# A kernel's instruction order from a new list scheduler: measured latencies, overlap, the shared port, and a local search

## The chip, the cores and the metric

One core of a Trainium2 chip. The metric is device microseconds of one execution; most executions of one kernel agree within 0.3%. All runs compared below are in the fast state, at a granted TensorE clock of 1.00, but for one repeat that ran once and whose state is therefore unknown.

## The reference

Four residual blocks over `x` of shape (1, 2048, 512), all bfloat16: linear attention with a softmax feature map, then a gated feed-forward, and both again.

```python
def A(x, wqkv, w_phi, wo):                    # 32 heads of 16
    q, k, v = split_heads(x @ wqkv)
    phi = lambda t: concat([softmax(t @ w_phi), softmax(-(t @ w_phi))])
    kv, z = phi(k).T @ v, phi(k).sum(over s)
    return merge_heads((phi(q) @ kv) / (phi(q) @ z + 1e-6)) @ wo
def B(x, W_gate, W_up, W_down):               # F = 1376
    return (relu(x @ W_gate) * (x @ W_up)) @ W_down
x = x + A(layernorm(x)); x = x + B(layernorm(x))
x = x + A(layernorm(x)); x = x + B(layernorm(x))
```

## The kernel before

The kernel writes a list of 3691 operations with reads and writes. A scheduler puts them into one fixed order per engine; waits on semaphores are then derived from the dependences. The engines are in order, so an operation whose data is late holds all that follows on its engine.

```python
class Program:
    ...                                   # the kernel sets SYNC_LAT = 120, SAME_LAT = 60
    DMA_FIXED = 2000.0
    DMA_BW = 240.0
    TRIALS = 6
    def schedule(self):
        ...
        noise = [[rng.uniform(0.92, 1.08) for _ in ops] for _ in range(self.TRIALS)]
        for weight in self.ORDER_WEIGHTS:
            prio = [weight * o.idx - rank[o.idx] - o.boost for o in ops]
            for _ in range(self.PASSES):
                start, finish, order = self._forward(prio)
                span = self._replay(order, noise)      # mean over six noisy replays
                ...
    def _forward(self, prio):
            ...
            if o.is_dma:                  # every DMA, a transpose too, shares one queue
                q_free = max(st + self.DMA_FIXED * 0.35, q_free) + o.dma_bytes / self.DMA_BW
                finish[i] = q_free + self.DMA_FIXED * 0.65
```

A layer's attention first runs the K/V stage (key and value projections, the softmax normalisation on GpSimd, and the sums that give `kv`; in the first layer up to about 55 us), then turns to the "num" stage (`phi(q) @ kv`) and the output projection. A tile is 128 of the 2048 rows: "tile 10" is `yT` of tile 10, "`oT` 4" the attention output of tile 4.

The DMA transposes are 92 in all. Each layer-normalised tile of 128 rows is transposed from `ytile` into `yT`, each attention output from `osb` into `oT` (the first few `yT` tiles are transposed on TensorE instead). The next matmul that reads the tile cannot start before the whole transpose has landed.

```python
    def dma_tr(self, fn, reads, writes, name):
        o = self.prog.dma("sp", fn, reads, writes, 131072, name)
        o.dur = 1190.0
        return o
    ...                                       # K and V projections of tile tt
    op("pe", ... e.matmul(k.pb[bank][:], k.yT[:, ic, tt * 128:(tt + 1) * 128], W[:, ic, :], ...)
    ...                                       # attention tile t: transpose, output projection
    self.dma_tr(lambda e: e.dma_start_transpose(k.oT[:, ob, :, :], k.osb[:, b, :]), ..., f"{tag} otr {t}")
    op("pe", ... e.matmul(k.pb[bank][:], k.oT[:, ob, c, :], k.wo_p[:, c, :], ...)
```

The softmax here doesn't subtract the row's maximum and nothing guards it: scores larger than these inputs give would overflow.

Of the kernel before, what the change touches and what calls it, by code (L numbers as in the profile page):

```python
# [24 lines left out]
class Op:  # L25
    __slots__ = ("idx", "eng", "fn", "reads", "writes", "dur", "is_dma", "queue",
                 "dma_bytes", "deps", "order_deps", "dset", "start", "finish", "cnt", "name", "boost")

    def __init__(self, idx, eng, fn, reads, writes, dur, name="", is_dma=False, queue=None, dma_bytes=0):
        self.idx = idx  # L30
        self.eng = eng
        self.fn = fn
        self.reads = reads
        self.writes = writes
        self.dur = dur
        self.name = name
        self.is_dma = is_dma
        self.queue = queue
        self.dma_bytes = dma_bytes
        self.deps = []  # L40
        self.order_deps = []
        self.start = None
        self.finish = None
        self.cnt = None
        self.boost = 0.0


class Program:
    SYNC_LAT = 500.0
    SAME_LAT = 500.0  # L50
    DMA_FIXED = 2000.0
    DMA_TAIL = 1300.0
    ORDER_WEIGHTS = (5.0, 10.0, 20.0, 30.0)
    PASSES = 12
    TRIALS = 6
    DMA_BW = 240.0
    DMA_ISSUE = {"sp": 650.0, "act": 650.0, "pool": 1100.0}

    def __init__(self, nc, window=48, n_dma_sems=48):
        self.nc = nc  # L60
        self.ops = []
        self.window = window if isinstance(window, dict) else {e: window for e in ENG_NAMES}
        self.n_dma_sems = n_dma_sems

    def op(self, eng, fn, reads=(), writes=(), dur=100.0, name=""):
        assert eng in ENG_NAMES
        o = Op(len(self.ops), eng, fn, list(reads), list(writes), float(dur), name)
        self.ops.append(o)
        return o

    def dma(self, eng, fn, reads=(), writes=(), nbytes=0, name=""):
        assert eng in QUEUE_OF
        o = Op(len(self.ops), eng, fn, list(reads), list(writes), self.DMA_ISSUE[eng], name,
               is_dma=True, queue=QUEUE_OF[eng], dma_bytes=nbytes)
        self.ops.append(o)
# [38 lines left out]
    def schedule(self):  # L114
# [9 lines left out]

        def lat(a, b):
            if a.is_dma:
                return self.DMA_TAIL + self.SYNC_LAT
            if a.eng == b.eng:
                return 0.0 if a.eng == "pe" else self.SAME_LAT
            return self.SYNC_LAT  # L130

        rank = [0.0] * n
        for o in reversed(ops):
            rank[o.idx] = o.dur + max([rank[q] + lat(o, ops[q]) for q, _ in self.succ[o.idx]], default=0.0)
        rng = random.Random(1)
        noise = [[rng.uniform(0.92, 1.08) for _ in ops] for _ in range(self.TRIALS)]
        best = None
        for weight in self.ORDER_WEIGHTS:
            prio = [weight * o.idx - rank[o.idx] - o.boost for o in ops]
            for _ in range(self.PASSES):  # L140
                start, finish, order = self._forward(prio)
                span = self._replay(order, noise)
                if best is None or span < best[0]:
                    best = (span, start, finish, order)
                prio = [t - o.boost for t, o in zip(self._backward(start, finish), ops)]
        _, start, finish, order = best
        self.makespan = max(finish)
        for o in ops:
            o.start, o.finish = start[o.idx], finish[o.idx]
        self.order = [ops[i] for i in order]  # L150
        return self.order


    def _forward(self, prio):
        ops, succ = self.ops, self.succ
# [5 lines left out]
        place = {}  # L161
# [5 lines left out]
        q_free = 0.0  # L167
        first = {e: 0 for e in ENG_NAMES}
# [3 lines left out]
        start, finish, order = [0.0] * n, [0.0] * n, []  # L172
        nxt = {e: None for e in ENG_NAMES}
        dirty = set(ENG_NAMES)
        while len(order) < n:
            for e in dirty:
                lst = pending[e]
                while first[e] < len(lst) and done[lst[first[e]]]:
                    first[e] += 1
                lim = first[e] + self.window[e]  # L180
                nxt[e] = min([(max(free[e], t), prio[i], i) for i, t in avail[e].items() if place[i] < lim], default=None)
            dirty = set()
            keys = [k for k in nxt.values() if k is not None]
            assert keys, "scheduler deadlock"
            st, _, i = min(keys)
            o = ops[i]
            start[i] = st
            free[o.eng] = st + o.dur
            if o.is_dma:
                q_free = max(st + self.DMA_FIXED * 0.35, q_free) + o.dma_bytes / self.DMA_BW  # L190
                finish[i] = q_free + self.DMA_FIXED * 0.65
            else:
                finish[i] = st + o.dur
            done[i] = True
            del avail[o.eng][i]
            dirty.add(o.eng)
            order.append(i)
            for q, is_data in succ[i]:
                e = ops[q].eng
                npred[q] -= 1  # L200
                if is_data:
                    ready[q] = max(ready[q], finish[i] + (self.SAME_LAT if o.eng == e else self.SYNC_LAT))
                if npred[q] == 0:
                    avail[e][q] = ready[q]
                    dirty.add(e)
        return start, finish, order


    def _replay(self, order, noise):
        ops = self.ops  # L210
        total = 0.0
        for f in noise:
            free = {e: 0.0 for e in ENG_NAMES}
            fin = [0.0] * len(ops)
            q_free = 0.0
            for i in order:
                o = ops[i]
                t = free[o.eng]
                for d in o.deps:
                    t = max(t, fin[d] + (self.SAME_LAT if ops[d].eng == o.eng else self.SYNC_LAT))  # L220
                free[o.eng] = t + o.dur * f[i]
                if o.is_dma:
                    q_free = max(t + self.DMA_FIXED * 0.35, q_free) + o.dma_bytes / self.DMA_BW * (3 * f[i] - 2)
                    fin[i] = q_free + self.DMA_FIXED * 0.65 * (5 * f[i] - 4)
                else:
                    fin[i] = free[o.eng]
            total += max(fin)
        return total / len(noise)


    def _backward(self, start, finish):
        ops, succ = self.ops, self.succ
# [12 lines left out]
        for _ in range(n):  # L245
            for e in dirty:
                nxt[e] = min([(-min(late[i] - (finish[i] - start[i]) + ops[i].dur, free[e]), -finish[i], i) for i in avail[e]], default=None)
# [3 lines left out]
            out[i] = free[o.eng] = -k - o.dur  # L251
            avail[o.eng].remove(i)
            dirty.add(o.eng)
            for d in o.deps + o.order_deps:
                e = ops[d].eng
                nsucc[d] -= 1
                lat = 0.0 if d not in o.dset else self.SAME_LAT if e == o.eng else self.SYNC_LAT
                late[d] = min(late[d], out[i] - lat)
# [110 lines left out]
class Kernel:  # L369
    def __init__(self, nc, A_x, A_wqkv, A_w_phi, A_wo, B_W_gate, B_W_up, B_W_down, out):  # L370
        self.nc = nc
        self.prog = Program(nc, window=WINDOW)
        self.prog.SYNC_LAT = 120.0
        self.prog.SAME_LAT = 60.0
        self.prog.DMA_ISSUE = {"sp": 450.0, "act": 500.0, "pool": 1100.0}
# [10 lines left out]
    def op(self, eng, fn, reads, writes, dur, name=""):  # L386
        return self.prog.op(eng, fn, reads, writes, dur, name)

    def dma(self, eng, fn, reads, writes, nbytes, name=""):
        return self.prog.dma(eng, fn, reads, writes, nbytes, name)  # L390

    def dma_tr(self, fn, reads, writes, name):
        o = self.prog.dma("sp", fn, reads, writes, 131072, name)
        o.dur = 1190.0
# [53 lines left out]
    def setup(self):  # L448
# [24 lines left out]
        def ldx(t0, t1, after=()):  # L473
            dma("sp", lambda e: e.dma_start(k.x_sb[:, t0:t1, :], xv[:, t0:t1, :]), list(after), [r("x", t) for t in range(t0, t1)], 131072 * (t1 - t0) if t1 > t0 + 1 else 96000, f"dma x{t0}")
        dma("sp", lambda e: e.dma_start(k.phi_c[:], A_w_phi.rearrange("(kc hl) d f -> (hl d) kc f", hl=8)), [], [r("phi_c")], 16384, "dma phi")
        for ic in range(NC):
            dma("act", (lambda ic: lambda e: e.dma_start(wk_n[:, ic, :], A_wqkv[ic * 128:(ic + 1) * 128, 512:1024]))(ic), [], [R_wkn[ic]], 96000, f"dma wk{ic}")
# [4 lines left out]
        dma("sp", lambda e: e.dma_start(k.wv_p[:], wqkv_v[:, :, 1024:1536]), first, [r("wv", ic) for ic in range(NC)], 524288, "dma wv")  # L482
# [3 lines left out]
        o.dur = 7000.0  # L486
# [92 lines left out]
    def ln(self, t, tag, on_act=False, pe_bank=None, stats=True, copy_act=False):  # L579
# [4 lines left out]
        if tag == "L0" and t > 3:  # L584
# [6 lines left out]
            else:  # L591
                op(how, lambda e: e.tensor_scalar(k.ytile[:, yb, :], k.x_sb[:, t, :], k.rstd[:, t, :], k.nmr[:, t, :], op0=ALU.mult, op1=ALU.add), dep, dst, 407 if how == "dve" else 2090, f"{tag} apply {t}")
        else:
            op("dve", lambda e: e.tensor_scalar(k.ytile[:, yb, :], k.x_sb[:, t, :], k.mv[:, t, 0:1], k.rstd[:, t, :], op0=ALU.subtract, op1=ALU.mult),
               [r("x", t), r("mv", t), r("rstd", t)], [r("yt", yb)], 407, f"{tag} apply {t}")
# [30 lines left out]
    def knorm(self, t, tag):  # L626
# [6 lines left out]
        for eng, s0, s1 in parts:  # L633
# [5 lines left out]
               (1930 if s1 - s0 == 2 else 980) if eng == "pool" else 1050, f"{tag} phik {t} {s0}")  # L639
# [56 lines left out]
    def num(self, t, nring, wring, tag):  # L696
# [3 lines left out]
        for gb in range(3):  # L700
# [18 lines left out]
           RN, [r("zm", b, 0), r("zm", b, 1)], 222 if sm == "dve" else 310, f"{tag} zm {t}")  # L719
        op(sm, lambda e: e.tensor_tensor(k.zd[:, b, :], k.zm[:, b, 0:32], k.zm[:, b, 32:64], ALU.add), [r("zm", b, 0), r("zm", b, 1)], [r("zd", b)], 190 if sm == "dve" else 270, f"{tag} zd {t}")  # L720
# [4 lines left out]
           RN + [r("zr", b)], [r("ab", b, 0), r("ab", b, 1)], 222 if sm == "dve" else 310, f"{tag} ab {t}")  # L725
# [4 lines left out]
           RN + [r("ab", b, 0), r("ab", b, 1)], [r("tsc", b)], 690, f"{tag} tsc {t}")  # L730
        op(sm, lambda e: e.tensor_tensor(k.osb[:, b, :], k.tsc[:, b, 0:512], k.tsc[:, b, 512:1024], ALU.add),  # L731
           [r("tsc", b)], [r("osb", b)], 418 if sm == "dve" else 1160, f"{tag} o {t}")
# [239 lines left out]
```

## Time and profile before

| | before |
|---|---|
| time, median of 3 runs | 391.79 us (391.71 to 392.03) |
| span of the profiled run, clock | 390.3 us, 1.00 |
| TensorE: 2331 matmuls at their pace (estimate from start-to-start gaps) | 373.1 us |
| TensorE stalls: start-to-start gaps less the pace | 11.3 us |

The busy share of TensorE (97%) includes each matmul's drain, so I count stalls instead: the time between the starts of two consecutive matmuls, less the pace of the first (216 ns for 512 columns, 109 for 256, 63 for 144, 56 for 128 and 129). By stretch this gives 5.7 us in the first 20 us, 1.6 from 20 to 50, 1.3 from 50 to 60, 1.2 from 60 to 80, 0.2 from 80 to 240, 1.2 from 240 to 270, 0.1 after.

From the page of the kernel before: the span, the TensorE row (busy us, share, instructions), and the chain of work that ended last.

```profile
span 390.3 us, 6397 instructions
...
PE 379.4 (97%) x2331; PEld 208.0 (53%) x2331; DVE 272.0 (70%) x547; ACT 206.6 (53%) x389; POOL 168.5 (43%) x284
...
PE 88%; POOL 4%; ACT 3%; DMA 2%; DVE 1%; issue 1%; ACTq 0%; POOLq 0%
```

The waits of TensorE in the kernel before (who waited for whom: us in total, times, longest):

```profile
PE ps L509 <- DMA hT<-in_A_wqkv_dram: 3.6, 2, 3.2
PE ps L617 <- ACT yT L605: 1.0, 1, 1.0
...
PE ps L663 <- POOL expk L634: 0.6, 1, 0.6
PE ps L706 <- ACT numbf L366: 0.5, 1, 0.5
...
PE ps L758 <- DMA yT<-ytile: 0.2, 1, 0.2
```

From the groups of the kernel before, GpSimd's normalisation in the K/V stages of both layers (count | busy us, mean ns | idle before it and its releaser):

```profile
L634 POOL TENSOR_TENSOR expk<-expk,rZk 128x1024 bf16<-128x1024 bf16 (+1 forms) x32 | 59.5, 1878 | 37.1 <-DVE rZk L631 19.7
```

### The profile page before, as it was taken

Reading aid. Unit: us, or ns where it says so; the run is one execution under the profiler, and the core shown is the slowest. Engines: PE = TensorE matmul, PEld = TensorE weight load, DVE = VectorE, ACT = ScalarE, POOL = GpSimd, SP = SyncE. Lnnn points to the kernel's source line nnn. Section 1 sums busy time; section 2 is a strip of 40 time slices with the busy share of each in tenths; the row PEclk is TensorE's granted clock in tenths of the full one; section 3 lists DMA queues with packets and bytes.
Section 4 is the critical chain, followed back from the end, with each engine's and each line's share of the span. In section 5 each row is a group of like instructions: output and inputs, shape, how many; then the busy total and the mean of one; then the engine's idle time right before and its main releaser. Section 6 shows DMA issues by size and latency. Waiting matters only on the chain.

```text
span 390.3 us, 6397 instructions
## 1 busy us (share of the span) xinstructions
PE 379.4 (97%) x2331; PEld 208.0 (53%) x2331; DVE 272.0 (70%) x547; ACT 206.6 (53%) x389; POOL 168.5 (43%) x284
## 2 busy tenths in 40 slices
PE   5999989999999999999999999999999999999997
PEld 3445554667644544444444457567774554444444
DVE  4999978877766888866766777897986776232222
ACT  5898859834633404533453484985563462553340
POOL 5499936641724363372244543584553242100000
DMA  6833682311311322401000110132323132100002
GB/s 179 228 67 71 191 299 53 69 40 32 53 40 27 43 55 44 84 10 28 14 15 0 27 29 3 40 80 57 55 55 69 27 42 67 29 14 27 17 12 67
DMA packets 61663, 23.01 MB, mean 59 GB/s; under 512 B 53472, under 2 KB 60608, under 8 KB 61632
## 3 DMA queue, kind: packets, MB, share of 16 engines
q1 hardware_dynamic: 60912, 22.02, 24.4%
q10 hardware_dynamic: 720, 0.59, 0.5%
q8 instruction: 18, 0.29, 0.3%
q14 instruction: 13, 0.11, 0.1%
HBM read 7.91 MB, written 2.10 MB: 26 GB/s over the span
## 4 chain that ended last, share of the span: by engine, by line
PE 88%; POOL 4%; ACT 3%; DMA 2%; DVE 1%; issue 1%; ACTq 0%; POOLq 0%
PE ps L758 39%; PE ps L785 19%; PE ps L617 7%; PE ps L737 7%; PE ps L690 6%; PE ps L706 4%; PE ps L663 3%; PE ps L648 2%; POOL expk L634 2%; ACT expq L693 2%; DVE stats L551 1%; DMA x_sb<-in_A_x_dram 1%; DMA hT<-in_A_wqkv_dram 1%; ACT expk L620 1%; POOL rstd L576 1%
## 5 line engine op out<-in xcount | busy, mean ns | idle before, releaser
L758 PE MATMUL ps<-yT,Wg 128*128 128x512 bf16 (+3 forms) x440 | 130.1, 337 | 0.5 <-DMA yT<-ytile 0.2
L758 PE MATMUL ps<-yT,Wu 128*128 128x512 bf16 (+3 forms) x440 | 129.6, 336 | 0.0
L760 ACT ACTIVATE gate_sb<-ps 128x512 bf16<-128x512 f32 (+3 forms) x110 | 55.9, 512 | 105.3 <-PE ps L758 102.9
L785 PE MATMUL ps<-Wd,hT 128*128 128x512 bf16 (+2 forms) x363 | 106.8, 373 | 0.0
L634 POOL TENSOR_TENSOR expk<-expk,rZk 128x1024 bf16<-128x1024 bf16 (+1 forms) x32 | 59.5, 1878 | 37.1 <-DVE rZk L631 19.7
L758 PEld LDWEIGHTS ps<-yT,Wg 128*128 128x128 bf16 (+1 forms) x440 | 43.4, 100 | 33.8 <-issue 1.1
L758 PEld LDWEIGHTS ps<-yT,Wu 128*128 128x128 bf16 (+1 forms) x440 | 43.7, 100 | 32.6 <-ACT expk L765 0.2
L767 DVE TENSOR_TENSOR hT<-gate_sb,expk 128x512 bf16<-128x512 bf16 (+3 forms) x73 | 29.8, 409 | 37.9 <-ACT expk L765 33.0
L785 PEld LDWEIGHTS ps<-Wd,hT 128*128 128x128 bf16 (+1 forms) x363 | 35.3, 98 | 36.6 <-DVE x_sb L787 0.6
L551 DVE BATCH_NORM_STATS2 stats<-x_sb 128x6 f32<-128x512 bf16 x64 | 42.6, 682 | 5.5 <-DMA x_sb<-in_A_x_dram 5.1
L366 ACT ACTIVATE numbf<-ps 128x432 bf16<-128x432 f32 x64 | 33.1, 536 | 19.5 <-PE ps L706 19.4
L629 DVE TENSOR_REDUCE Zk<-expk 128x64 f32<-128x1024 bf16 x32 | 37.7, 1194 | 5.7 <-ACT expk L620 5.4
L731 POOL TENSOR_TENSOR osb<-tsc 128x512 bf16<-128x512 bf16 x28 | 32.5, 1162 | 19.9 <-DVE tsc L726 17.8
L737 PE MATMUL ps<-wo_p,oT 128*128 128x512 bf16 x128 | 39.8, 379 | 0.0
L770 DVE TENSOR_TENSOR hT<-gate_sb,ps 128x512 bf16<-128x512 bf16 (+2 forms) x37 | 22.7, 613 | 20.8 <-PE ps L758 19.6
L693 ACT ACTIVATE expq<-ps 128x1024 bf16<-128x1024 f32 (+1 forms) x40 | 32.6, 861 | 7.3 <-PE ps L690 7.0
L765 ACT ACTIVATE expk<-ps 128x512 bf16<-128x512 f32 (+3 forms) x73 | 36.1, 497 | 0.1
L706 PE MATMUL ps<-kvbd,expq 128*128 128x144 bf16 x256 | 35.0, 226 | 0.5 <-ACT numbf L366 0.5
L620 ACT ACTIVATE expk<-ps 128x512 bf16<-128x512 f32 x44 | 23.9, 598 | 21.5 <-PE ps L617 21.2
L690 PE MATMUL ps<-yT,Wqp 128*128 128x512 bf16 x128 | 34.6, 379 | 0.6 <-ACT expq L693 0.5
L787 DVE TENSOR_TENSOR x_sb<-x_sb,ps 128x512 bf16<-128x512 bf16 (+1 forms) x33 | 22.0, 669 | 18.8 <-PE ps L785 18.4
L559 POOL TENSOR_TENSOR rstd<-rv,mhalf 128x1 f32<-128x1 f32 (+1 forms) x53 | 31.9, 607 | 2.9
(73 smaller groups left out, 429.2 us busy)
## 6 DMA issues: line engine op xcount, KB each, us to landing
out_dram<-x_sb SPq DMA_DIRECT2D x15, 128.0 KB, 1.7
x_sb<-in_A_x_dram SPq DMA_DIRECT2D x3, 512.0 KB, 6.2
Wu<-in_B_W_up_dram SPq DMA_DIRECT2D x4, 344.0 KB, 5.9
Wg<-in_B_W_gate_dram SPq DMA_DIRECT2D x4, 344.0 KB, 5.5
Wd<-in_B_W_down_dram SPq DMA_DIRECT2D x5, 256.0 KB, 6.9
yT<-ytile SPq DMA_TRANSPOSE x60, 2.5
hT<-in_A_wqkv_dram ACTq DMA_DIRECT2D x4, 128.0 KB, 3.1
x_sb<-in_A_x_dram SPq DMA_DIRECT2D x4, 128.0 KB, 3.7
```

What stands on the lines that cost most here:

```text
L366: return e.activation(out, in_, ACT.Copy) if hasattr(e, "activation") else e.tensor_copy(out, in_)
L551: op("dve", (lambda t: lambda e: e.bn_stats(k.stats6[:, t, :], k.x_sb[:, t, :]))(t), [r("x", t)], [r("st", t)], 685, f"{tag} stats {t}")
L629: op("dve", lambda e: e.tensor_reduce(k.Zk[:, zb, :], k.expk[:, t, :, :].rearrange("p s (h f) -> p (s h) f", f=16), AX.X, ALU.add), [r("ex ...
L634: op(eng, (lambda s0, s1: lambda e: e.tensor_tensor(k.expk[:, t, s0:s1, :].rearrange("p s (h f) -> p (s h) f", f=16), k.expk[:, t, s0:s1, ...
L690: op("pe", (lambda c, ic, bank: lambda e: e.matmul(k.pb[bank][:], k.Wqp[:, ic, c * 128:(c + 1) * 128], k.yT[:, ic, st * 512:(st + 1) * 512 ...
L693: op("act", (lambda c0, s, b0: lambda e: e.activation(k.expq[:, st, c0:c0 + w, s, :], k.ps[:, b0:b0 + w, :], ACT.Exp, scale=(1.0 - 2.0 * s ...
L706: op("pe", (lambda s, c, j, g0, bank: lambda e: e.matmul(k.pb[bank][:, j * GW:(j + 1) * GW], k.expq[:, st, c, s, tt * 128:(tt + 1) * 128], ...
L737: op("pe", (lambda c, bank: lambda e: e.matmul(k.pb[bank][:], k.oT[:, ob, c, :], k.wo_p[:, c, :], start=(c == 0), stop=(c == NC - 1)))(c, ...
L758: op("pe", (lambda bank, W, ic, fc, Mf: lambda e: e.matmul(k.pb[bank][0:Mf, 0:n], W[:, ic, fc * 128:fc * 128 + Mf], k.yT[:, ic, c0:c0 + n] ...
L760: op("act", (lambda Mf, gb, gs: lambda e: e.activation(k.gate_sb[0:Mf, gs, 0:n], k.pb[gb][0:Mf, 0:n], ACT.Relu))(Mf, gb, gs), [self.RP[gb] ...
L765: op("act", (lambda Mf, ub, tu: lambda e: e.activation(k.expk[0:Mf, tu, 0, 0:n], k.pb[ub][0:Mf, 0:n], ACT.Copy))(Mf, ub, tu), [self.RP[ub] ...
L785: op("pe", (lambda fc, Kf, u, c0, bank, m0, m1: lambda e: e.matmul(k.pb[bank][:, m0:m1], k.hT[0:Kf, u, c0:c0 + 128], k.Wd[0:Kf, fc, m0:m1] ...
```

## The change

The intent is a better fixed order. No operation is added or removed: the model behind the scheduler has separate latencies per engine, lets consecutive operations of one engine overlap, keeps VectorE and GpSimd apart on their shared port, and charges a DMA transpose a fixed 2.45 us outside the DMA queue. The noisy replays are gone. Sixteen recorded steps of a local search then improve the order in the model.

```diff
-    SYNC_LAT = 500.0
-    SAME_LAT = 500.0
-    DMA_FIXED = 2000.0
-    DMA_TAIL = 1300.0
+    TO = {"act": 36.0, "dve": 34.0, "pool": 86.0, "pe": 57.0, "sp": 27.0}
+    OVERLAP = {"act": 107.0, "dve": 82.0, "pool": 40.0, "pe": -163.0, "sp": 0.0}
+    PORT_POOL = 143.0
+    DMA_BW = 235.0
+    DMA_START = 1250.0
+    DMA_TAIL = 650.0
+    TR_ISSUE, TR_LAND = 1190.0, 2450.0
-    TRIALS = 6
+    STEPS = (287922835, 372001363, ...)          # 16 seeds
 ...
-        noise = [[rng.uniform(0.92, 1.08) for _ in ops] for _ in range(self.TRIALS)]
-                span = self._replay(order, noise)
+                span, start, finish = self._forward(prio)
 ...
+        best = self.first_order()
+        for seed in self.STEPS:
+            best = self.step(best, seed)
 ...
-            if o.is_dma:
-                q_free = max(st + self.DMA_FIXED * 0.35, q_free) + o.dma_bytes / self.DMA_BW
-                finish[i] = q_free + self.DMA_FIXED * 0.65
+            if o.lat is None:
+                q_free = max(st + self.DMA_START, q_free) + o.dma_bytes / self.DMA_BW
+                fin = q_free + self.DMA_TAIL
             else:
-                finish[i] = st + o.dur
+                fin = st + o.lat
 ...
-        o = self.prog.dma("sp", fn, reads, writes, 131072, name)
-        o.dur = 1190.0
+        o = self.prog.dma("sp", fn, reads, writes, 131072, name, self.prog.TR_LAND)
+        o.occ = self.prog.TR_ISSUE
```

## The prediction

> **What bounds the kernel now.** TensorE. The page gives PE 97% busy over a 390.3 us span, but that overstates it: each matmul record includes its drain (379 ns for 512 columns). Start to start, the trace's 512-column matmuls stand 216 ns apart, 256-column ones 109, 144-column ones 63, 129-column ones 56. My estimate: the 2331 matmuls at these paces need about 373 us. The other 17 us: 3.2 us before the first matmul (weights landing), 2.5 us after the last (residual, store), about 11.5 us of stalls, by start-to-start gaps less the pace:
> - 0 to 20 us: about 5.7 us, some 2 us of them 128-column matmuls 107 ns apart rather than 56. The Trainium skill, page "TensorE: Matmul & The Clock Gate", section "Part 1: The HAM clock gate", gives 106.7 and 55.6 ns for a cold and a warm array; the trace agrees, and no order mends that. Another 1.1 us is the wait at 11.3 us for ScalarE's copy of yT.
> - 20 to 80 us: about 4.5 us, in the K/V stage and where it turns into the "num" stage.
> - 240 to 260 us: about 1.2 us, the same turn in the second layer.
> - Elsewhere nothing: the table by stretches shows PE full from 80 to 240 us and from 260 to the tail.
>
> **What the change does.** No instruction is added or removed; each engine's order moves. The old scheduler used flat latencies and averaged over noisy durations; the new one has measured latencies, overlap within an engine and the port that VectorE and GpSimd share, and improves its order over 16 recorded steps. Only stalls can be won: about 7 us if all that is not cold clock or first load went; 2% is 7.8 us.
>
> **What I expect of each place.**
> - K/V stage: GpSimd is full from 21 to 52 us, its 16 normalisations (1.9 us each) on the chain. The first starts only at 21.07 because VectorE runs seven statistics (0.6 us each) before the reciprocal it needs. The new order puts that reciprocal after two of them, and the normalisation before the mean/variance group: it should start near 16.7 us. GpSimd's work from there sums to about 34 us, so its last normalisation should end near 50.5 rather than 52.0: 1 to 1.5 us won, if VectorE (also full from 13 to 51 us) keeps up. The port locks stay: a 0.4 us VectorE apply took 1.92 us at 26.4 us, beside GpSimd; the skill's page "SBUF — State Buffer", section "Who interferes with whom", calls it an exclusive lock, and the trace agrees.
> - First 13 us: about 0. The second K tile still waits for the last yT copy, now behind both exponentials, and V for its weights.
> - Turns near 55 and 245 us: ScalarE (exponentials 1.0 us, evacuations 0.5 us) paces PE; 0.5 to 1.5 us in all.
> - Feed-forward stages and tail: nothing to win, a few tenths to lose.
>
> Sum: 1.5 to 3 us. Predicted time **389.3 us**, range 387.2 to 391.1. Chances: faster by over 2% 0.01, within 2% 0.97, slower by over 2% 0.02.
>
> **What would show it right or wrong.** GpSimd's first normalisation near 16.7 us, last ending 50 to 51 us; the stall between 20 and 80 us down from 4.5 to 2 to 3.5 us; at 240 to 260 us below 1 us; 80 to 240 us as before. If the first normalisation moves and the stall stays, VectorE or ScalarE was the limit.
>
> **What would make it wrong.** A single searched order may be fitted to its model: one wait 0.3 us longer than modelled holds an in-order engine, and PE has no slack: then 391 to 393. Or the search mends the first 20 us too; then 387.

## The result and the profile after

The changed kernel takes 396.18 us (median of 4, 395.13 to 396.77) against 391.75 us (391.69 to 392.03) for the kernel before on the same chip: a ratio of 1.0105, 95% interval 1.0083 to 1.0126. Here and below a ratio is the mean time of one kernel's fast runs over that of the other's of the same rounds, so it is not quite the ratio of the medians quoted.

So the order got slower by about 4 us (1%, clear of the noise), where 2.5 us less was predicted. Stalls of TensorE by stretch, in us, from the matmul starts of each trace (43 of the 2331 matmul records are missing in the first trace of the changed kernel and were filled in at their pace; a second trace misses none):

| stretch, us | before | after | after, second trace |
|---|---|---|---|
| 0 to 20 | 5.7 | 6.6 | 5.9 |
| 20 to 50 | 1.6 | 1.7 | 1.8 |
| 50 to 60 | 1.3 | 2.6 | 2.6 |
| 60 to 80 | 1.2 | 3.1 | 2.9 |
| 80 to 240 | 0.2 | 0.4 | 0.4 |
| 240 to 270 | 1.2 | 1.6 | 1.2 |
| all | 11.3 | 16.0 | 14.9 |

From the page of the changed kernel, the same rows as before:

```profile
span 395.0 us, 6307 instructions
...
PE 377.8 (96%) x2288; PEld 206.9 (52%) x2331; DVE 266.2 (67%) x547; ACT 207.6 (53%) x389; POOL 168.2 (43%) x284
...
PE 80%; DVE 6%; POOL 5%; DMA 5%; ACT 2%; issue 2%; SPq 0%; POOLq 0%; DVEq 0%
PE ps L789 37%; PE ps L816 19%; PE ps L648 7%; PE ps L768 6%; PE ps L721 4%; PE ps L737 3%; DMA oT<-osb 3%; PE ps L694 2%; POOL expk L665 2%; DVE stats L582 2%; PE ps L679 1%; DMA yT<-ytile 1%; DMA x_sb<-in_A_x_dram 1%; POOL rstd L590 1%; ACT expq L724 1%
```

In the last chain TensorE's share falls from 88% to 80%, and the transposes `oT<-osb` and `yT<-ytile` have entered it. The waits of TensorE in the changed kernel say the same:

```profile
PE ps L540 <- DMA hT<-in_A_wqkv_dram: 4.1, 2, 3.2
PE ps L789 <- DMA oT<-osb: 2.2, 2, 1.6
PE ps L721 <- ACT expq L724: 1.4, 2, 0.9
PE ps L679 <- DMA yT<-ytile: 0.9, 1, 0.9
PE ps L768 <- DMA oT<-osb: 0.8, 1, 0.8
...
PE ps L737 <- DVE kvbd L710: 0.7, 1, 0.7
```

About 3.9 us of waiting for transposes (3.0 in the second trace) stands where the kernel before had 0.2. (L789 is a gate/up matmul and reads no `oT`. In the second trace, which misses no record, one matmul of the output projection, L768, stands ahead of it and carries the wait; in the first trace that record is missing, so the wait went to its successor.) The line of the second trace:

```profile
PE ps L768 <- DMA oT<-osb: 2.0, 2, 1.4
```

The chain of the changed kernel in order of time, from 30 to 80 us, shows each transpose with its time from issue to landing (start us, us, what; most lines left out):

```profile
34.00 3.56 DMA yT<-ytile
37.55 0.05 issue
37.60 1.05 PE ps L679 x4
...
51.57 0.56 DVE rZk L662
52.13 2.75 DVE expk L665 x2
54.88 0.97 DVE kvbd L705 x2
...
60.49 3.66 DMA oT<-osb
64.16 0.04 issue
64.20 1.04 PE ps L768 x4
```

The same query from 72 to 80 us has the largest of them:

```profile
73.40 1.15 POOL osb L762
74.55 0.03 POOL ab L753
74.58 4.10 DMA oT<-osb
78.68 0.27 issue
78.95 0.71 PE ps L789 x5
```

These transposes took 3.56, 3.66 and 4.10 us. The model charges 2.45 us, which is right for the median: 2.44 us in the trace before and 2.45 us in the trace after. But 13 of the 92 took more than 2.7 us in each of the two traces, so as a group the change did not make them slower. It made them matter. (Not all are the same tiles: 12, `oT` 4 and `oT` 5 of the last layer are late in both traces; 10, 13 and `oT` 0 land after 2.40 to 2.51 us in the kernel before.)

GpSimd's normalisation after the change:

```profile
L665 POOL TENSOR_TENSOR expk<-expk,rZk 128x1024 bf16<-128x1024 bf16 (+1 forms) x32 | 59.3, 1865 | 34.6 <-DVE rZk L662 31.6
```

The first one starts at 17.65 us (21.07 before), but in the first layer its last normalisation ends at about 54.3 us instead of 52.0. The 31.6 us of waiting for VectorE's reciprocal (19.7 before) are those of the whole kernel; between 13 and 56 us the wait view gives 3.4 us in three waits, and no such wait before. In that stretch VectorE itself waits 2.3 us for ScalarE's exponentials (not at all before).

### Why some transposes are late

The DMA view of the changed kernel from 74.5 to 78.7 us, which covers the 4.10 us transpose (40 equal slices; then queues with packets, MB and share; then issues with their median time to landing):

```profile
DMA  0000000000006999988000000000000001799996
GB/s 0 0 0 0 0 0 0 0 0 0 0 10 139 217 227 205 215 180 210 3 0 0 0 0 0 0 0 0 0 0 0 0 0 29 163 232 227 212 207 146
...
q1 hardware_dynamic: 1052, 0.26, 30.4%
q8 instruction: 1, 0.02, 1.4%
issues: line engine op xcount, KB each, median us to landing
oT<-osb SPq DMA_TRANSPOSE x2, 3.3
```

The data of the transpose moves between about 75.7 and 76.5 us; then the DMA engines are almost idle for 1.5 us. In that gap there is one packet of the queue named "instruction". It is 16 KB long, starts at 76.44 us and takes 0.92 us. The trace's landing records show how the transpose ended: fifteen of the sixteen increments of its semaphore came between 76.84 and 76.99 us, and the sixteenth at 78.68. The packet records show where it was held. The data is followed by 32 packets of 4 bytes (by my reading, the increments): 30 start by 76.65 us, the last two at 77.34 and 77.35, just as the instruction packet ends. The 1.3 us from there to the landing no record explains. In the seven traces named below, 40 transposes have a last increment that stands alone by more than 0.5 us; in 36 of them a 4-byte packet starts within 10 ns of the end of an instruction packet, of 16 or of 8 KB.

The Trainium skill explains how to read that. Its page "DMA: Bandwidth & Descriptors", section "Why a DMA increments its semaphore by 16 and not by 1", says that a DMA runs on up to 16 engines that finish independently, each adding one increment after its own data; the trace agrees, sixteen increments for each transpose. The page "Runtime: NRT & Kernel Launch", section "Instruction fetch mechanics", says that a sequencer fetches its program through its own DMA queue, in blocks of 16 KiB or 256 instructions. The trace agrees here too: 18 packets of 16 KB for TensorE's 4662 matmul and weight-load instructions, one for every 259. (The trace does not name that queue's engine; that it is TensorE's is my reading of this count, and the run `after_fill64` below tests it.)

Over seven traces (before, after twice, after_fill64, after_nosteps, nosteps_land3000 and best_order) the association is nearly complete. Of 64 transposes with a 16 KB fetch starting 0 to 2.1 us after their issue, 61 took more than 2.7 us. Of 445 with no instruction packet from 1.0 us before the issue to 2.45 us after it, 3 did; all three are attention tile 0, which is issued behind the loads of the feed-forward weights. In the remaining 135, with a smaller packet or one at the edge of the interval, 41 did. (The five other traces give the same picture: 36 of 39, and 5 of 330.) Attention tile 0 goes with those loads instead, though no run moved them on purpose. It is late, by 0.7 us or more, in the six of all twelve traces in which the last of these loads lands 2.6 to 3.4 us after its issue, and on time in the six where that load lands at most 1.8 us after it.

### What the order did with its slack

I replayed both orders under the new model (model values, not times). The order of before takes 389.05 us and the new one 388.04, so the whole modelled gain is 1.0 us. Measured against this model, TensorE ends 0.9 us late in the kernel before and 6.7 us late in the changed one (5.5 us in the second trace). Slack is how much later than 2.45 us after its issue a transpose may land before its first reader on TensorE is delayed in the model. Before, 6 of the 92 transposes have less than 0.5 us; after, 20 have.

A second replay gives each transpose the landing that its own trace shows instead of 2.45 us. The order of before then takes 389.1 us in the model, 0.1 more than nominal; the changed order takes 392.6 (392.0 with the second trace), 4.6 us more. So in the model the late landings alone turn a gain of 1.0 us into a loss of 3.5, of the 4.4 measured.

### The profile page after: what moved, and what is told of

Its sections match the earlier page's. It is cut to its first block, busy times and chain, and to the rows that moved or that the text cites. A ratio compares the mean times of both kernels' runs of the same rounds, so it can differ in the third digit from the quotient of the medians.

```text
span 395.0 us, 6307 instructions
## 1 busy us (share of the span) xinstructions
PE 377.8 (96%) x2288; PEld 206.9 (52%) x2331; DVE 266.2 (67%) x547; ACT 207.6 (53%) x389; POOL 168.2 (43%) x284
## 4 chain that ended last, share of the span: by engine, by line
PE 80%; DVE 6%; POOL 5%; DMA 5%; ACT 2%; issue 2%; SPq 0%; POOLq 0%; DVEq 0%
PE ps L789 37%; PE ps L816 19%; PE ps L648 7%; PE ps L768 6%; PE ps L721 4%; PE ps L737 3%; DMA oT<-osb 3%; PE ps L694 2%; POOL expk L665 2%; DVE stats L582 2%; PE ps L679 1%; DMA yT<-ytile 1%; DMA x_sb<-in_A_x_dram 1%; POOL rstd L590 1%; ACT expq L724 1%
## 5 line engine op out<-in xcount | busy, mean ns | idle before, releaser
L789 PE MATMUL ps<-yT,Wg 128*128 128x512 bf16 (+3 forms) x435 | 118.3, 336 | 2.5 <-DMA oT<-osb 2.2
L789 PE MATMUL ps<-yT,Wu 128*128 128x512 bf16 (+3 forms) x434 | 118.2, 336 | 0.4
L791 ACT ACTIVATE gate_sb<-ps 128x512 bf16<-128x512 f32 (+3 forms) x110 | 55.8, 511 | 85.8 <-PE ps L789 75.8
L816 PE MATMUL ps<-Wd,hT 128*128 128x512 bf16 (+2 forms) x353 | 99.2, 373 | 0.6
L665 POOL TENSOR_TENSOR expk<-expk,rZk 128x1024 bf16<-128x1024 bf16 (+1 forms) x32 | 59.3, 1865 | 34.6 <-DVE rZk L662 31.6
L789 PEld LDWEIGHTS ps<-yT,Wu 128*128 128x128 bf16 (+1 forms) x440 | 43.2, 100 | 34.1 <-ACT expk L796 0.7
L789 PEld LDWEIGHTS ps<-yT,Wg 128*128 128x128 bf16 (+1 forms) x440 | 43.0, 100 | 33.3 <-ACT gate_sb L791 1.0
L798 DVE TENSOR_TENSOR hT<-gate_sb,expk 128x512 bf16<-128x512 bf16 (+2 forms) x73 | 27.3, 375 | 35.1 <-ACT expk L796 30.4
L796 ACT ACTIVATE expk<-ps 128x512 bf16<-128x512 f32 (+2 forms) x73 | 35.9, 496 | 20.5 <-PE ps L789 20.1
L768 PE MATMUL ps<-wo_p,oT 128*128 128x512 bf16 x123 | 37.7, 379 | 1.0 <-DMA oT<-osb 0.8
L589 POOL TENSOR_SCALAR rv<-mv 128x1 f32<-128x1 f32 (+1 forms) x53 | 12.0, 227 | 57.0 <-DVE mv L584 56.6
```

The costliest lines, as they stand in the source:

```text
L665: op(eng, (lambda s0, s1: lambda e: e.tensor_tensor(k.expk[:, t, s0:s1, :].rearrange("p s (h f) -> p (s h) f", f=16), k.expk[:, t, s0:s1, ...
L768: op("pe", (lambda c, bank: lambda e: e.matmul(k.pb[bank][:], k.oT[:, ob, c, :], k.wo_p[:, c, :], start=(c == 0), stop=(c == NC - 1)))(c, ...
L789: op("pe", (lambda bank, W, ic, fc, Mf: lambda e: e.matmul(k.pb[bank][0:Mf, 0:n], W[:, ic, fc * 128:fc * 128 + Mf], k.yT[:, ic, c0:c0 + n] ...
L791: op("act", (lambda Mf, gb, gs: lambda e: e.activation(k.gate_sb[0:Mf, gs, 0:n], k.pb[gb][0:Mf, 0:n], ACT.Relu))(Mf, gb, gs), [self.RP[gb] ...
L796: op("act", (lambda Mf, ub, tu: lambda e: e.activation(k.expk[0:Mf, tu, 0, 0:n], k.pb[ub][0:Mf, 0:n], ACT.Copy))(Mf, ub, tu), [self.RP[ub] ...
L816: op("pe", (lambda fc, Kf, u, c0, bank, m0, m1: lambda e: e.matmul(k.pb[bank][:, m0:m1], k.hT[0:Kf, u, c0:c0 + 128], k.Wd[0:Kf, fc, m0:m1] ...
```

## The experiments

Theory L: what was lost was lost to late transposes on an order that left them no slack. Theory F adds that they are late because of instruction fetches. Rivals: the loss is spread over everything the scheduler moved; the search overfitted; other parts of the model are wrong; the late tiles are late for reasons of their own. The runs after_free6, after_shift96, h1 and h2 were on one chip (before: 391.65 us), before_free6, after_fill64, after_nosteps and best_order on another (391.85), after_again and nosteps_land3000 on a third (391.89).

### after_free6: six transposes taken out of the way

The first readers of the six tiles that stalled TensorE read a resident weight instead, so the result is wrong. The order and the transposes themselves stay.

```diff
+FREE = {'A0 k 10', 'A0 k 12', 'A0 k 13', 'A0 wo 0', 'A0 wo 4', 'A2 wo 5'}
-    e.matmul(k.pb[bank][:], k.oT[:, ob, c, :], k.wo_p[:, c, :], ...)
+    e.matmul(k.pb[bank][:], k.Wkp[:, c, 0:128] if f"{tag} wo {t}" in FREE else k.oT[:, ob, c, :], k.wo_p[:, c, :], ...)
```

(The K projection is edited likewise, and the dependences on the six transposes are dropped after scheduling.)

> Order unchanged from the changed kernel; six tiles' first TensorE readers (K of tiles 10, 12, 13; output projection of tiles 0 and 4 in layer 1, of tile 5 in layer 2) read weights already on chip instead of the transposed tile, so they wait for no transpose; the result is wrong on purpose. Theory L (transposes that land 1 to 2.4 us later than modelled meet an order with no slack): the stalls before these six, 1.0+0.3+1.0+1.5+0.55 = 4.4 us in the trace, go, and the time falls from 396.2 to between 391.2 and 393. Rival G (GpSimd and VectorE starve in the K/V stage because LayerNorm work moved later): at most 1.3 us of that lies there, so 395 or more. Rival S (a slower start): unchanged, 395.5 or more.

Measured: 392.54 us (392.43 to 392.64, 5 runs), ratio 1.0019, interval 1.0005 to 1.0033. Of the 1.05% that the change cost, 0.86% is gone. In the waits of TensorE no transpose is left, though `oT` 0 and 4 still land late in this trace (3.69 and 4.10 us); the stalls from 60 to 80 us are 0.8 us. What stays is the end of the K/V stage, 2.9 us between 50 and 60 us (1.3 before).

### before_free6: the same edit in the kernel before

> Control for the first run of six freed transposes: the kernel before, with the same edit (the first readers of transposed tiles 10, 12 and 13, of the attention tiles 0 and 4, and of tile 5 of the last layer's attention read a resident weight instead, so the result is wrong on purpose). Theory L (late landings cost something only where the order left no slack): the trace of before shows no TensorE wait for a transposed tile above 0.2 us, so nothing can be won: 391.2 to 392.0 us, ratio 0.999 to 1.001. Rival R (the edit itself makes the kernel cheaper, whatever the order, because six waits and six reads are gone): some 3 us won here as well, 388 to 389.5 us.

Measured: 391.86 us (391.06 to 391.9, 4 runs), ratio 0.9996, interval 0.9983 to 1.0009, and stalls of 11.2 us as before. The same tiles are worth nothing where the order leaves slack, so the edit is not cheaper by itself. Tile 12, `oT` 4 and `oT` 5 of the last layer are late here as in the kernel before (3.32, 3.95 and 3.99 us); nobody waits for them.

### after_shift96: instruction fetches moved, first try

192 waits that are already met at the head of TensorE's program, 96 instructions in the trace.

```diff
+        if e == "pe":
+            for _ in range(192):
+                eng.wait_ge(sems["pool"], 1)
```

> 96 waits that are already met stand at the head of TensorE's program, where it idles for the first 3.2 us; nothing else changes. They only move the points at which TensorE's instruction stream crosses a 16 KB fetch, about 96 instructions (5 to 8 us in the early stages) earlier. Theory L, in the form that the late transposes are those in flight while a fetch is on the DMA engines: the stall of 1.5 us before output projection 4 goes (under 0.3 us), that before projection 5 of layer 2 too, and others of 0.5 to 1.6 us may come at whatever tight transposes the fetches meet now; total 393.5 to 397. Rival (the late transposes are late for their own sake, by queue position or by weights in the queue): the same tiles stall by the same amounts, 396.2 within 0.6.

Measured: 401.67 us (401.01 to 402.24, 4 runs), ratio 1.0252. A miss: the head waits alone held the first matmul to 11.5 us instead of 3.2. The stalls ahead of `oT` 4 and of tile 5 in the last layer did vanish, and in the trace that is kept one of 0.9 us came up at 152.5 us; `oT` 0 stayed late (3.75 us, a stall of 1.1). But with everything shifted by 8 us against the loads, this run proves nothing alone.

### after_fill64: instruction fetches moved, second try

The same idea where it costs nothing: one further instruction after each of the first 64 matmuls of the key and value projections, which last 216 ns each.

```diff
             ins = o.fn(eng)
             ...
+            if e == "pe" and o.name[:4] in ("A0 k", "A0 v") and o.name[4] == " " and n_fill < 64:
+                n_fill += 1
+                for _ in range(2):
+                    eng.wait_ge(sems["pool"], 1)
```

> The changed kernel, order and data untouched, with 64 further instructions (pairs of waits that are long met) between the first 64 matmuls of 512 columns of the key and value projections, so that every later 16 KB instruction fetch of TensorE comes 64 instructions, some 4 to 5 us, earlier against the work. Theory F (a transpose is late because an instruction fetch runs while it is in flight): the fetches move off tile 12 and 13's transposes (38.0 us), attention tile 4's (74.6) and tile 5's of the last layer (265.0), so the stalls of 1.5 us before the output projection of tile 4 and 0.55 us in the last layer go, those of tile 13 too; tile 10's may stay. Total 392.5 to 395 us, if the added waits hide behind the 216 ns matmuls; the sum of stalls above 0.25 us between 60 and 270 us falls from 4.9 us to below 3.3 us. Rival G (the transposes of these tiles are late for a reason of their own place in the order, such as the queue or the tile's own data): the same tiles stay slow, the same stalls stay at the same instructions, 396 us or more.

Measured: 396.2 us (395.92 to 398.85, 6 runs), ratio 1.0121, interval 1.0101 to 1.0142. The trace has 64 more TensorE records, and the fetches come earlier: at 35.0 instead of 38.7 us, 70.5 instead of 76.4, 258.6 instead of 265.2. The places behave as theory F says. Tiles 12 and 13, `oT` 4, and tile 5 of the last layer, the four that had met a 16 KB fetch, are all on time, and the 1.5 us stall is gone. `oT` 0 is on time too, but it had met no instruction packet, so it says nothing for theory F. The waits of TensorE in this run (L773 is the output projection, L684 the K projection):

```profile
PE ps L773 <- DMA oT<-osb: 2.6, 3, 1.6
PE ps L684 <- DMA yT<-ytile: 1.5, 1, 1.5
```

And its chain around the new largest one, 256 to 263 us:

```profile
257.23 4.21 DMA oT<-osb
261.44 0.04 issue
261.48 0.39 PE ps L773
```

This is `oT` 3 of the last layer, with the fetch of 258.6 us starting 1.36 us after its issue; `oT` 3 of the first layer is now late as well (3.13 us), and tile 10 later than ever (4.07 us, fetch 1.71 us after issue). They stall TensorE for 1.7, 0.9 and 1.6 us. So my sum was wrong: stalls above 0.25 us between 60 and 270 us add to 4.1 us, not below 3.3, and the total did not fall. I had looked only at what the fetches would leave, not at what they would hit. But the same order and data with the fetches elsewhere stall at other tiles, and of the six late tiles only tile 10 is late again. For those four the cause goes with the fetch, not with the tile. `oT` 0 goes with the weight loads, as said above, and tile 10 met only two 8 KB instruction packets in the changed kernel; these two made 2.0 of the 4.4 us of stalls. With 20 of 92 transposes short of slack, moving the fetches only chooses who pays.

The DMA view from 73.3 to 77.2 us in this run covers the transpose that took 4.10 us in the changed kernel (`oT` 4, issued here at 73.37). Its issue line:

```profile
oT<-osb SPq DMA_TRANSPOSE x2, 2.4
```

There is no instruction packet in this stretch.

### after_again: the same kernel once more

> The changed kernel once more, unaltered, for a second trace. Theory F (the late transposes come from instruction fetches, whose place in the program is fixed): the same tiles are late again and the same stalls appear, 0.5 us or more before the key projection of tile 10 and 1 us or more before the output projections of tiles 0 and 4, each within 0.5 us of its size in the first trace. Rival C (chance collisions on the memory): other tiles are late. Time 395 to 397 us.

Measured: 395.54 us, one run. All 13 late transposes of the first trace are late again, plus one more. The stalls: 0.47 us at tile 10 (1.02 in the first trace), 0.87 at tile 13 (0.29), 0.82 at `oT` 0 (1.01), 1.53 at `oT` 4 (1.54). Three of my limits were missed narrowly (0.47 for 0.5, 0.82 for 1, and a change of 0.55 us at tile 10), but chance collisions would not pick the same 13 of 92 tiles. A cause that lies in the order itself would repeat as well; it is after_fill64 that tells the two apart.

### h1_before_kv and h2_after_kv: halves of the order

A stored order replaces the scheduler. In h1 the 577 operations of the set-up, the K/V stage and the first weight loads stand in the order they had before, in the places they hold in the changed kernel; in h2 it is the other way round.

```diff
-        self.setup_search()
-        best = self.first_order()
-        ...
+        seq = struct.unpack(f"<{len(self.ops)}H", zlib.decompress(base64.b85decode(ORDER)))
+        self.order = [self.ops[i] for i in seq]
```

> The changed order, with the set-up and K/V stage of layer 1 and the weight loads (577 operations) in the old order among themselves. Theory L: the stalls at K 10 and K 13 and the one at projection 0 go (2.3 us), and most of the slower start (1 us); the ones at projection 4 of layer 1 (1.5 us, if the fetch still meets it) and 5 of layer 2 (0.55 us) stay: 392.3 to 394.3. Rival G or S alone (all the loss is in the K/V stage or the start): 391.0 to 391.9.

Measured: 394.03 us (393.7 to 394.75, 4 runs), ratio 1.0060. The stall before the output projection of tile 4 stays, 1.5 us from 75.8 us on.

> The old order, with set-up and K/V stage of layer 1 and weight loads in the changed order among themselves. Theory L: the start and K 10, K 13 stalls stay (about 2.3 us over the old kernel), projection 0 is absorbed by the old order's slack of 1.4 us, no stalls of over 0.6 us after 65 us: 393 to 395. Rival G or S alone: 395.5 to 396.5.

Measured: 393.93 us (393.59 to 394.66, 4 runs), ratio 1.0057. Each half costs about 2.3 us and the two add up to about the whole (4.7 against 4.4 us). The loss is at several places, not in one stage.

### after_nosteps: without the search

```diff
-        for seed in self.STEPS:
-            best = self.step(best, seed)
```

> The changed kernel without its 16 search steps: the list scheduler's own best order under the new model. The model gives it 390.4 us where the searched order has 388.0 and the order of before 389.1. Theory S (the search overfitted the model: it took out the slack): clearly better than the changed kernel, 391 to 393 us, at most 0.6 per cent over before. Theory L2 (the new list scheduler itself leaves no slack, searched or not; 18 transposes have under 0.5 us of slack in this order, 20 in the searched one, 6 in that of before): as late against its model as the searched order, so 394.5 to 398 us.

Measured: 396.5 us (396.22 to 397.62, 4 runs), ratio 1.0117, interval 1.0102 to 1.0131. The search is not to blame: without it the kernel is no faster. It improved the model by 2.3 us (390.4 to 388.0), of which the chip shows 0.3 us by medians, within the spread. The list scheduler itself leaves little slack. Replayed with its own trace's landings this order takes 392.8 us in the model, 2.5 more than nominal (4.6 for the searched one): what the search gained in the model, it lost again to late landings.

### nosteps_land3000: one constant

```diff
-    TR_ISSUE, TR_LAND = 1190.0, 2450.0
+    TR_ISSUE, TR_LAND = 1190.0, 3000.0
```

> The changed scheduler without its 16 search steps, with one constant of its model changed: a transpose is charged 3.0 us from issue to landing instead of 2.45. Replayed with 2.45 us, this order takes 390.2 us in the model, as the one without search steps does (390.4), but it leaves 7 transposes with less than 0.5 us of slack where that one left 18. Theory L (late landings on an order without slack): the same model time and more slack give a faster kernel, 392.5 to 395 us against 396.5, and the stalls of over 1 us before the output projections of the first tiles go. Rival Q (what is lost lies in the other new latencies, the port rule or the order of the engines, and the charge for a transpose hardly matters): 396 us or more.

Measured: 393.78 us (393.5 to 394.1, 6 runs), ratio 1.0047, interval 1.0026 to 1.0068. Replayed with 2.45 us both orders take the same model time (390.2 and 390.4 us), but the one with more slack runs 2.7 us faster (by the ratios, 0.7%). Replayed with its own trace's landings this order takes 390.4 us in the model, 2.4 less than the one without the constant. Its lateness against the model at the end is 1.0 us, as in the kernel before; without the constant it was 4.9. But the trace of after_nosteps is of its slowest run (397.62 us), and 1.3 us of the difference are stalls in the first 20 us (6.6 against 5.4), where no transpose is waited for. It is one order against one other. Thirteen transposes are late here too. The only wait of TensorE for a transpose of 0.2 us or more is

```profile
PE ps L787 <- DMA yT<-ytile: 0.5, 1, 0.5
```

### best_order: slack bought on purpose

A stored order again, from a search of 700 s on each of four starts under the same latencies. Its objective is the mean of twelve replays with random late landings instead of the one nominal replay. The edit is the stored order of h1 with other contents.

> A stored order from a longer search under the same latencies and the same dependences, judged by the mean of twelve replays in which each transpose has a chance of 15 per cent of landing 0.6 to 1.6 us late and the first loads land 0.3 to 0.8 us late. Those replays give 387.5 us as their mean, where the order of before gets 391.2 and that of the change 393.9. Theory L (what the changed kernel lost it lost to late landings, and slack against them wins it back): 387.5 to 390 us, faster than before by 0.4 to 1 per cent. Rival M (the model is wrong elsewhere as well, so that any order found with it is slower than the order of before): 392 us or more.

Measured: 391.1 us (390.71 to 391.5, 5 runs), ratio 0.9982, interval 0.9970 to 0.9994. It beats both kernels, but by 0.2% over before, far less than the 387.5 to 390 us expected. Nineteen transposes are late and cost little (0.6 us in the model, replayed with the landings of its own trace); the TensorE waits of 0.2 us or more for them are

```profile
PE ps L704 <- DMA yT<-ytile: 0.3, 1, 0.3
...
PE ps L683 <- DMA oT<-osb: 0.2, 1, 0.2
```

So late landings are no longer what costs, and the promise still was not kept. The order is worth 386.1 us in the nominal model, 2.9 us less than the order of before, and TensorE ends 2.6 us late on the chip (0.9 for before). That lateness is 0.6 us at the first matmul, 1.0 at 8 us, 1.3 at 80 us, 1.7 at 200 us and 2.5 at 380 us: it comes in small pieces. Why the model is optimistic there I did not settle. Theory L holds for the loss; that slack alone would then win 2 us was wrong.

## Why the prediction was wrong

- **"Sum: 1.5 to 3 us" of gain.** This is the term that failed. I counted where the new order could take stalls away and gave the new order credit for it. The replay shows that even in the change's own model the gain was 1.0 us. What failed is the step from "only stalls can be won" to that sum: it left TensorE's waits for transposes out of account (0.2 us before). They became 3.9 us, and the late landings cost several times the gain: the six tiles of after_free6 account for 0.86% of the 1.05%, some 3.4 us.
- **"Feed-forward stages and tail: nothing to win, a few tenths to lose."** Wrong between 60 and 80 us, where attention tiles, gate and up matmuls share TensorE: stalls went from 1.2 to 3.1 us, because output projections 0 and 4 were moved right up to the nominal landing of their transposes.
- **"The stall between 20 and 80 us down from 4.5 to 2 to 3.5 us."** It went from 4.1 to 7.4 us.
- **GpSimd's first normalisation near 16.7 us, last ending 50 to 51.** The first came at 17.65, so the mechanism was read rightly. The last ended at 54.3: the new order moved second-group layer norms on VectorE later, and GpSimd waited for rZk. The prediction had named its condition, "if VectorE keeps up". It did not: in the chain VectorE's Zk, rZk, expk and kvbd run up to the start of the num matmuls. But VectorE was not the only limit: in after_free6, where tiles 10, 12 and 13 hold nobody, the last normalisation ends at 52.9 us, so about 1.4 of the 2.3 us of delay came with the late transposes. Stalls from 50 to 60 us, the turn where 0.5 to 1.5 us was to be won together with the one near 245, doubled instead, 1.3 to 2.6 us, and after_free6 leaves them. How much of the final time that part costs by itself was not tried.
- **240 to 260 us below 1 us, 80 to 240 us as before.** Roughly right at 0.7 us (1.1 before); but tile 5 of the last layer added 0.55 us at 267 us, just past that window, and 0.2 in the second trace. 80 to 240 us: 0.2 and 0.4 us.
- **"One wait 0.3 us longer than modelled holds an in-order engine, and PE has no slack: then 391 to 393."** The mechanism was named and shown, but mis-sized and mis-weighted. It was not one wait of 0.3 us but five of 0.3 to 1.5 us, since 13 of 92 transposes are 0.5 to 2.4 us longer than their median, and it should have been the central case.
- What was within reach before the run: the profile before already held 13 late transposes with a single wait of 0.2 us on any of them. That is a statement about slack, and asking what the new order does to that slack could have turned the sign.

Still open: the 50 to 60 us stretch (each half of the order has it alone, 3.2 us in h1 and 2.6 in h2), the first 20 us (5.7 us of stalls before, 5.9 to 6.6 after), and the slow drift of best_order against its model.

## What to carry to other kernels

When its model is fitted to medians, a scheduler can place readers right at the median landing (here 20 of 92 within 0.5 us), and what lands later then stalls an in-order engine. Charge an asynchronous operation nearer its late case (here 3.0 instead of 2.45 us gave an order 2.7 us faster on the chip at equal model time), or score the order over perturbed landings. Before trusting a tighter order, count how many waits have slack below the known spread, not just the makespan. A sporadic late DMA need not be noise: check whether the same transfers are late in a second trace and what else is on the DMA engines at that moment.

## What the Trainium skill lacked or had wrong

- "Runtime: NRT & Kernel Launch", section "Instruction fetch mechanics", calls the cost of crossing a 16 KiB boundary "mostly hidden". Here the sequencer itself may well hide it, but a transpose in flight does not: 61 of 64 transposes with a fetch starting 0 to 2.1 us after their issue landed after 2.7 us or more, up to 4.9 us, against a median of 2.45. A fetch packet takes 0.9 to 1.7 us.
- "DMA: Bandwidth & Descriptors" explains the sixteen increments but gives no figure for what an instruction fetch costs a transfer in flight: in the 4.10 us transpose fifteen increments came within 0.15 us and the sixteenth 1.7 us later. In 5 of the 13 late transposes of the changed kernel (6 of 13 before) the last increment stands alone by more than 0.5 us; in the others all sixteen are late, and why those differ no run shows.
- No page gives the cost on TensorE of a wait that is already met: ahead of its first instruction, 192 of them (96 instructions of two, 0.11 us apart in the trace) delayed the first matmul by 8.3 us, while 128 of them spread behind 216 ns matmuls between 8 and 27 us left the stalls of that stretch at 3.0 us, as in the second trace of the changed kernel.
